# Three Newton rounds of the row norms moved from VectorE to GpSimd, for four of five gate batches

## The chip, the cores and the metric

The kernel runs on one core of one Trainium2 chip. The metric is device time in microseconds of one execution; the kernel before took 1360.23 us, the median of three runs (1359.64 to 1362.73). Engine names in the rows: PE is TensorE, PEld its weight loads, DVE is VectorE, ACT is ScalarE, POOL is GpSimd, SP is SyncE, which here issues DMAs.

## The reference

Three layers follow one another on 4608 tokens of width 512: attention inside chunks of 64 tokens, a mixture of eight experts in which each token goes to one, and a wide layer with a swish.

```python
scores = scale * np.matmul(q_c, k_c.transpose(0, 1, 2, 4, 3))
attn = softmax(scores)                       # rows of 64
x = concat_heads(np.matmul(attn, v_c))       # (4608, 512)

xn = x / (np.linalg.norm(x, axis=-1, keepdims=True) + 1e-06)
en = expert_emb / (np.linalg.norm(expert_emb, axis=-1, keepdims=True) + 1e-06)
logits = xn @ en.T / tau
expert_idx = np.argmax(logits, axis=1)
gate_w = softmax(logits)[np.arange(N), expert_idx]
out[mask] = gate_w[mask, None] * (np.maximum(x[mask] @ w1[e], 0.0) @ w2[e])   # per expert e

h = out @ w_in
result = (h * (1.0 / (1.0 + np.exp(-1.702 * h)))) @ w_out
```

The change concerns one quantity: 1 / (norm of x + 1e-6) for each token, by which its eight logits are scaled.

## The kernel before

Tokens are worked in 36 tiles of 128. The first stage, the attention, ends some 218 us into the span; the expert layer and the wide layer follow and fill the rest. In the attention stage a loop over n (L1143) is a software pipeline: in step n it makes scores and softmax of tile n (`emit_S`, `max_S`, `exp_S`), transposes the probabilities of tile n-1 (`emit_PT`, `evac_PT`), multiplies tile n-2 by v (`emit_PV`, `emit_x`), sums the squares of tile n-3 on ACT (`emit_sq`) and writes tile n-3 out in two halves of 16 bits (`emit_X`). The order is written by hand: each engine executes its instructions in the order in which the code issues them, and an instruction that waits holds everything behind it on that engine.

On DVE a step has the row maxima `mx` (L378), the subtraction `P` (L381), on some steps a copy `xTa` (L476), the scale of a tile (`si_all`, `sx_all`, L442 and L447), its high half `xr` (L452), and the normalised output `x` (`rd`, L424 and L426, then L428). On ACT a step has four evacuations of transposed q or k (`kuT`, `quT`, L349), the squares `sq` of an `x` (L436), sometimes a copy `xTa` (L474), `PT` (L401) and the exponential of `P` (L388). On POOL a step has two instructions of 128x512: the scaling of `x` (L454) and the low half `xr` (L455).

Routing is done in five batches of 8, 8, 8, 6 and 6 tiles (`batches`, L479). When the last tile of a batch has been through `emit_X`, `norm(bi)` is put into the queue `todo`; `gate(bi)` follows it there when the logits of the last tile are there. Both are generators, and `drip(1)`, which stands at about ten places of a step, takes one piece out of the queue's head, so that these small instructions lie between the large ones. With `rate` 2 (steps 29 to 32) it takes two. `norm` turns the sums of squares `ss_all` of a batch (128 x 8 numbers, or 128 x 6) into `rn_all`: a first guess by an integer shift and a subtraction, three Newton rounds of three instructions (`rsqrt`, L215), a product that turns 1/norm into norm, the 1e-6, a reciprocal, and a scaling. All 16 of these are DVE instructions, and a drip stands between any two.

A generator that yields "pe" is set aside once:

```python
        if g in paused:
            n -= paused.pop(g)
            continue
        ...
        if next(g) == "pe":
            paused[g] = 8
```

The next call of `drip` takes the 8 off its own allowance of one or two, removes the entry and ends; the call after that takes the generator's next piece.

Of the kernel before, what the change touches and what calls it, by code (L numbers as in the profile page):

```python
# [12 lines left out]
I32 = mybir.dt.int32  # L13
U32 = mybir.dt.uint32
AF = mybir.ActivationFunctionType
ALU = mybir.AluOpType
# [18 lines left out]
def kernel(  # L35
# [13 lines left out]
    nc = tc.nc  # L49
# [102 lines left out]
    for t in vt:  # L152
# [15 lines left out]
        out=tri16, in_=ones16, pattern=[[1, 128]], compare_op=ALU.is_gt, fill=0.0,  # L168
# [19 lines left out]
    for m_, op_ in ((lt_m, ALU.is_lt), (le_m, ALU.is_le)):  # L188
        nc.vector.tensor_tensor(
            out=m_, in0=io_e.unsqueeze(1).to_broadcast([128, NE, NE]),  # L190
            in1=io_e.unsqueeze(2).to_broadcast([128, NE, NE]), op=op_,
# [23 lines left out]
    def rsqrt(y, t, a, ssc):  # L215

        nc.vector.tensor_scalar(t, ssc.bitcast(I32), 1, None, op0=ALU.logical_shift_right)
        yield
        nc.vector.tensor_scalar(
            y.bitcast(I32), t, -1.0, 1597463007.0, op0=ALU.mult, op1=ALU.add  # L220
        )
        yield
        for _ in range(3):
            nc.vector.scalar_tensor_tensor(
                out=a, in0=y, scalar=-0.5, in1=ssc, op0=ALU.mult, op1=ALU.mult
            )
            yield
            nc.vector.tensor_tensor(out=a, in0=a, in1=y, op=ALU.mult)
            yield
            nc.vector.scalar_tensor_tensor(  # L230
                out=y, in0=a, scalar=1.5, in1=y, op0=ALU.add, op1=ALU.mult
            )
            yield
# [245 lines left out]
    batches = [(0, 8), (8, 8), (16, 8), (24, 6), (30, 6)]  # L479
# [19 lines left out]
    def small(nm, n, dt=F32, w=None, bufs=1):  # L499
        t = att.tile([128, 8] if w is None else [128, 8, w], dt, tag="g_" + nm, name="g_" + nm, bufs=bufs)  # L500
        return t[:, 0:n]
# [3 lines left out]
    def norm(bi):  # L505
        t0, n = batches[bi]
        ssc, y = ss_all[:, t0:t0 + n], rn_all[:, t0:t0 + n]
        yield from rsqrt(y, small("t", n, I32), small("a", n), ssc)
        nc.vector.tensor_tensor(out=y, in0=y, in1=ssc, op=ALU.mult)
        yield  # L510
        nc.vector.tensor_scalar(y, y, 1e-6, None, op0=ALU.add)
        yield
        nc.vector.reciprocal(out=y, in_=y)
        yield
        isx = is_all[:, t0:t0 + n]
        nc.vector.tensor_scalar(
            isx.bitcast(I32), si_all[:, t0:t0 + n], float((BIAS - X_TOP) << 23), None, op0=ALU.add
        )
        yield
        nc.vector.scalar_tensor_tensor(  # L520
            out=y, in0=y, scalar=itau[:, 0:1], in1=isx, op0=ALU.mult, op1=ALU.mult
        )
        yield
# [603 lines left out]
    def end_X(t):  # L1127
        emit_X(t)
        for bi, (t0, nn) in enumerate(batches):
            if t == t0 + nn - 1:  # L1130
                todo.append(norm(bi))
# [698 lines left out]
```

## Time and profile before

| | |
|---|---|
| median of three runs | 1360.23 us |
| profiled execution, span | 1360.5 us, 1358.8 us |
| attention stage, 26 to 218 us: DVE, ACT, PE, POOL busy | 157.00, 159.02, 143.13, 96.64 us of 192 |
| 600 to 1350 us: PE busy | 728.49 us of 750 |
| mean granted TensorE clock | 0.979 |

A timeline row gives start, duration, engine, line, operation, and in brackets how long the engine sat idle before it and what ended that. Lines are those of the kernel before. Where two DVE instructions don't depend on each other, the second can start a little before the first one's end.

### The profile page before, as it was taken

How to read it: one execution, taken by the hardware profiler on the slowest of the kernel's cores; microseconds unless marked ns; L12 is line 12 of the kernel's file. 1: busy time of each engine (PE TensorE's matmuls, PEld its weight loads, DVE VectorE, ACT ScalarE, POOL GpSimd, SP SyncE). 2: the span in 40 equal slices, each digit the busy share in tenths (PEclk: the TensorE clock that was granted, in tenths of full speed). 3: DMA queues.
4: the chain of work that ended last, by engine and by line, in shares of the span. 5: the costliest groups of instructions: out<-in, count | busy, mean ns of one | idle time of the engine just before them, and what ended most of it. 6: DMA issues, size and time to landing. Idle time of an engine off the chain costs nothing. (4 is left out here: it accounts for less than half of the span.)

```text
span 1358.8 us, 35354 instructions
## 1 busy us (share of the span) xinstructions
PE 1245.2 (92%) x14192; PEld 1026.7 (76%) x14192; DVE 1052.1 (77%) x1872; ACT 729.4 (54%) x1301; POOL 716.5 (53%) x652
## 2 busy tenths in 40 slices
PE   6778767899999999999899999999999999999997
PEld 4656656677666666667588888888888888888886
DVE  4688888778988878886678696968787796968681
ACT  7899865235544545454454545545454545455453
POOL 1455543142544254543157575766667675757664
PEclk9999978999999999999999999999999999999999
DMA  9999634668655759876507253443526062534413
GB/s 196 228 246 227 158 136 123 187 180 235 181 184 160 212 164 276 252 230 159 150 5 214 63 164 117 125 156 92 189 34 220 28 196 85 156 125 124 156 39 118
DMA packets 218455, 213.63 MB, mean 157 GB/s; under 512 B 127320, under 2 KB 171352, under 8 KB 218272
## 3 DMA queue, kind: packets, MB, share of 16 engines
q1 hardware_dynamic: 204880, 184.17, 50.6%
q0 software_dynamic: 6000, 19.67, 4.2%
q10 hardware_dynamic: 7392, 7.36, 1.7%
q8 instruction: 114, 1.87, 0.6%
q14 instruction: 69, 0.57, 0.1%
HBM read 154.98 MB, written 36.52 MB: 141 GB/s over the span
## 5 line engine op out<-in xcount | busy, mean ns | idle before, releaser
L1536 PEld LDWEIGHTS <-wS 128*128 128x128 f16 x3024 | 296.4, 98 | 54.7 <-issue 16.2
L1029 PEld LDWEIGHTS <-w1HL 128*128 128x128 f16 x3744 | 215.5, 99 | 26.4 <-DVEq L962 9.4
L1029 PE MATMUL ph<-xTm,w1HL 128*128 128x128 f16 x3744 | 221.8, 221 | 14.3 <-DVEq L962 8.0
L1064 PE MATMUL py<-w2HL,hT 128*128 128x512 f16 x912 | 204.7, 379 | 6.1 <-DVEq L962 3.4
L1064 PEld LDWEIGHTS <-hT 128*128 128x128 f16 x936 | 90.0, 98 | 109.8 <-issue 9.5
L1089 ACT ACTIVATE y<-py,ysc 128x512 f16<-128x512 f32 x38 | 26.1, 687 | 142.6 <-DVE ysc L1086 142.6
L1004 POOL DMA_INDIRECT xg<-xs,id_i x39 | 42.9, 1100 | 109.4 <-DMA xTm<-xg 75.3
L1536 PEld LDWEIGHTS <-w2HL 128*128 128x128 f16 x864 | 84.5, 98 | 10.6
L1536 PEld LDWEIGHTS <-w1HL 128*128 128x128 f16 x864 | 84.5, 98 | 9.8
L454 POOL TENSOR_TENSOR x<-x,sx_all 128x512 f32<-128x512 f32 x33 | 34.3, 1039 | 107.5 <-DVE rd L424 49.1
L1256 POOL TENSOR_TENSOR wS<-d_f,wS 128x512 f16<-128x512 f32 x28 | 36.5, 1319 | 73.9 <-ACT wS L1255 43.8
L1562 ACT ACTIVATE zA<-zA 128x512 f32<-128x512 f32 x72 | 45.3, 629 | 54.0 <-DVE zA L1559 31.4
L1403 POOL TENSOR_TENSOR w1HL<-zA,w1HL 128x512 f16<-128x512 f32 x36 | 48.5, 1346 | 43.5 <-ACT w1HL L1399 43.5
L1396 DVE TENSOR_TENSOR zA<-zA 128x512 f32<-128x512 f32 x72 | 65.6, 911 | 1.2
L1037 DVE SCALAR_TENSOR_TENSOR hT<-ph,hT 128x512 f16<-128x512 f32 x78 | 51.4, 684 | 16.7 <-ACT hT L1036 16.5
L1036 ACT ACTIVATE hT<-ph 128x512 f16<-128x512 f32 x78 | 44.2, 593 | 31.1 <-PE ph L1029 31.0
L1536 PE MATMUL pd<-stg,wS 128*128 128x256 f16 x456 | 54.7, 272 | 5.2 <-ACT stgB L1399 5.2
L1686 POOL DMA_INDIRECT out_dram<-hT,idc x36 | 35.4, 983 | 35.8 <-ACT hT L1681 32.8
L1536 PE MATMUL pa<-stg,wS 128*128 128x256 f16 x432 | 51.8, 273 | 2.6 <-ACT stgB L1399 2.6
L1536 PE MATMUL pb<-stg,wS 128*128 128x256 f16 x408 | 49.0, 272 | 3.9 <-ACT stgB L1399 3.9
L1090 DVE SCALAR_TENSOR_TENSOR y<-py,ysc,y 128x512 f16<-128x512 f32 x38 | 28.5, 751 | 28.7 <-ACT y L1089 28.7
L349 ACT ACTIVATE kuT<-tp 64x512 f32<-64x512 f32 x72 | 45.2, 627 | 9.0 <-PE tp L344 8.1
(408 smaller groups left out, 3138.7 us busy)
## 6 DMA issues: line engine op xcount, KB each, us to landing
ring<-wod SPq DMA_DIRECT2D x63, 1024.0 KB
stg<-in_moe_w_dram SPq DMA_DIRECT2D x14, 1024.0 KB
stgB<-in_moe_w_dram SPq DMA_DIRECT2D x14, 1024.0 KB
ys<-y SPq DMA_DIRECT2D x39, 258.0 KB
vt<-in_v_dram SPq DMA_DIRECT2D x64, 144.0 KB
xs<-xr SPq DMA_DIRECT2D x36, 256.0 KB
raw_o<-in_moe_w_in_dram SPq DMA_DIRECT2D x16, 512.0 KB
raw_o<-in_moe_w_out_dram SPq DMA_DIRECT2D x16, 512.0 KB
```

Source lines behind the costliest of these rows:

```text
L349: lambda r=r, p=p, dst=dst: nc.scalar.activation(out=dst[:, :, r], in_=p[r * 64:(r + 1) * 64], func=AF.Copy)
L1004: nc.gpsimd.indirect_dma_start(out=xg[:, :], out_offset=None, in_=src, in_offset=bass.IndirectOffsetOnAxis(ap=id_i[:, i:i + 1], axis=0),)
L1029: nc.tensor.matmul(p[:, f % 4], wt[:, c, fs], xT[:, a, :], start=(c == 0 and a == 0 and wt is w1H), stop=(c == KD - 1 and wt is w1L),)
L1036: nc.scalar.activation(out=hi, in_=p, func=AF.Relu)
L1037: nc.vector.scalar_tensor_tensor(out=lo, in0=p, scalar=0.0, in1=hi, op0=ALU.max, op1=ALU.subtract)
L1064: nc.tensor.matmul(p, hT[:, a, :], wt[:, c, :], start=st, stop=sp)
L1256: nc.gpsimd.tensor_tensor(out=L_, in0=f, in1=H_, op=ALU.subtract)
L1396: nc.vector.tensor_tensor(out=o, in0=x, in1=p, op=op)
L1403: eng.tensor_tensor(out=lo, in0=x, in1=hi, op=ALU.subtract)
L1536: nc.tensor.matmul(dst, lhs(a, k, ab), rhs(b, k), start=first and ab == abs_[0] and k == 0 and m == 0, stop=(k == n - 1 and m == 2), skip_ ...
L1562: nc.scalar.activation(out=z, in_=z, func=AF.Sigmoid, scale=1.702 * 2.0 ** -G_EXP)
L1686: disjoint("out", nc.gpsimd.indirect_dma_start(out=out[:, :], out_offset=bass.IndirectOffsetOnAxis(ap=id_t[j][0][:, 2 * h + t, 0:1], axis= ...
```

## The change

For all batches the scaling factor `is_all` is made first instead of last. For the four first batches `norm` makes the first guess on DVE and then issues, in one piece, fifteen POOL instructions: `h` = -ss/2, three rounds of four (the fused DVE forms become separate ones), the product with `ss_all` and the 1e-6. Then it yields "pe", and the reciprocal and the scaling follow on DVE. The last batch keeps its Newton rounds on DVE.

```diff
     def norm(bi):
         t0, n = batches[bi]
         ssc, y = ss_all[:, t0:t0 + n], rn_all[:, t0:t0 + n]
-        yield from rsqrt(y, small("t", n, I32), small("a", n), ssc)
-        nc.vector.tensor_tensor(out=y, in0=y, in1=ssc, op=ALU.mult)
-        yield
-        nc.vector.tensor_scalar(y, y, 1e-6, None, op0=ALU.add)
-        yield
-        nc.vector.reciprocal(out=y, in_=y)
-        yield
         isx = is_all[:, t0:t0 + n]
         nc.vector.tensor_scalar(
             isx.bitcast(I32), si_all[:, t0:t0 + n], float((BIAS - X_TOP) << 23), None, op0=ALU.add
         )
+        yield
+        if bi + 1 < len(batches):
+            gp = nc.gpsimd
+            t, a, h = small("t", n, I32), small("a", n), small("h", n)
+            nc.vector.tensor_scalar(t, ssc.bitcast(I32), 1, None, op0=ALU.logical_shift_right)
+            yield
+            nc.vector.tensor_scalar(y.bitcast(I32), t, -1.0, 1597463007.0, op0=ALU.mult, op1=ALU.add)
+            gp.tensor_scalar(h, ssc, -0.5, None, op0=ALU.mult)
+            for _ in range(3):
+                gp.tensor_tensor(out=a, in0=h, in1=y, op=ALU.mult)
+                gp.tensor_tensor(out=a, in0=a, in1=y, op=ALU.mult)
+                gp.tensor_scalar(a, a, 1.5, None, op0=ALU.add)
+                gp.tensor_tensor(out=y, in0=y, in1=a, op=ALU.mult)
+            gp.tensor_tensor(out=y, in0=y, in1=ssc, op=ALU.mult)
+            gp.tensor_scalar(y, y, 1e-6, None, op0=ALU.add)
+            yield "pe"
+        else:
+            yield from rsqrt(y, small("t", n, I32), small("a", n), ssc)
+            nc.vector.tensor_tensor(out=y, in0=y, in1=ssc, op=ALU.mult)
+            yield
+            nc.vector.tensor_scalar(y, y, 1e-6, None, op0=ALU.add)
+            yield
+        nc.vector.reciprocal(out=y, in_=y)
         yield
```

On DVE before, the first batch's norm begins behind the high half of tile 7 (step 10); `g_t`, `g_a` and `rn_all` are the norm's, `rd`, `x` and `mx` the tiles':

```order
L217 TENSOR_SCALAR g_t<-ss_all 128x8
L219 TENSOR_SCALAR rn_all<-g_t 128x8
L424 TENSOR_SCALAR rd<-db 128x8
L224 SCALAR_TENSOR_TENSOR g_a<-rn_all,ss_all 128x8
L426 RECIPROCAL rd<-rd 128x8
L228 TENSOR_TENSOR g_a<-g_a,rn_all 128x8
L428 TENSOR_TENSOR x<-db,rd 128x2x4x64
L230 SCALAR_TENSOR_TENSOR rn_all<-g_a,rn_all 128x8
L224 SCALAR_TENSOR_TENSOR g_a<-rn_all,ss_all 128x8
L378 TENSOR_REDUCE mx<-sp_178 128x8
```

The same place of DVE in the changed kernel:

```order
L509 TENSOR_SCALAR is_all<-si_all 128x8
L516 TENSOR_SCALAR g_t<-ss_all 128x8
L424 TENSOR_SCALAR rd<-db 128x8
L518 TENSOR_SCALAR rn_all<-g_t 128x8
L426 RECIPROCAL rd<-rd 128x8
L428 TENSOR_TENSOR x<-db,rd 128x2x4x64
L534 RECIPROCAL rn_all<-rn_all 128x8
L536 SCALAR_TENSOR_TENSOR rn_all<-rn_all,itau,is_all 128x8
L378 TENSOR_REDUCE mx<-sp_178 128x8
```

The norm's reciprocal (L534) now stands in step 10, two instructions behind the piece that hands the rounds over (L518) and ahead of the next step's `mx`; before, it stood a step later. Batches two and three have the same order.

On POOL in the changed kernel, the place behind the low half of tile 7 (the names in brackets are the engines whose work the instruction waits for):

```order
L455 TENSOR_TENSOR xr<-x,xr 128x512 [waits DMAHW2_49,PE_49,Pool_49]
L519 TENSOR_SCALAR g_h<-ss_all 128x8
L521 TENSOR_TENSOR g_a<-g_h,rn_all 128x8 [waits DVE_49,Pool_49]
L522 TENSOR_TENSOR g_a<-g_a,rn_all 128x8 [waits Pool_49]
L523 TENSOR_SCALAR g_a<-g_a 128x8 [waits Pool_49]
L524 TENSOR_TENSOR rn_all<-rn_all,g_a 128x8 [waits Pool_49]
```

Two more such rounds, the product and the sum follow, each with the same wait, and then the scaling of tile 8 (L454). Before, L454 of tile 8 followed L455 of tile 7 directly.

On DVE before, the fourth batch (step 32, two pieces to a drip):

```order
L217 TENSOR_SCALAR g_t<-ss_all 128x6
L219 TENSOR_SCALAR rn_all<-g_t 128x6
L224 SCALAR_TENSOR_TENSOR g_a<-rn_all,ss_all 128x6
L228 TENSOR_TENSOR g_a<-g_a,rn_all 128x6
L424 TENSOR_SCALAR rd<-db 128x8
L230 SCALAR_TENSOR_TENSOR rn_all<-g_a,rn_all 128x6
L224 SCALAR_TENSOR_TENSOR g_a<-rn_all,ss_all 128x6
L426 RECIPROCAL rd<-rd 128x8
```

The same place in the changed kernel:

```order
L509 TENSOR_SCALAR is_all<-si_all 128x6
L516 TENSOR_SCALAR g_t<-ss_all 128x6
L518 TENSOR_SCALAR rn_all<-g_t 128x6
L424 TENSOR_SCALAR rd<-db 128x8
L534 RECIPROCAL rn_all<-rn_all 128x6
L536 SCALAR_TENSOR_TENSOR rn_all<-rn_all,itau,is_all 128x6
L426 RECIPROCAL rd<-rd 128x8
L428 TENSOR_TENSOR x<-db,rd 128x2x4x64
```

Here the norm's reciprocal stands ahead of the tile's own `rd` and `x`. The orders of PE, ACT and SP are the same in both kernels.

## Rows read from the trace of the kernel before

**Rows 1.** Windows: start:end, length, busy us by engine, clock, DMA share, GB/s.
```profile
26.00:218.00 192.00, 143.13 (x3223) 117.17 (x3221) 157.00 (x493) 159.02 (x296) 96.64 (x99) 0.90 0.89 200
600.00:1350.00 750.00, 728.49 (x6699) 635.51 (x6697) 567.66 (x761) 378.78 (x676) 464.83 (x400) 1.00 0.43 127
```
**Rows 2.** Timeline of ACT, step 11 and the beginning of step 12.
```profile
70.49 0.62 ACT L388 ACTIVATE P<-P 128x512 f32<-128x512 f32 x1
...
72.68 0.63 ACT L436 ACTIVATE sq<-x 128x512 f32<-128x512 f32 x1 [0.39 <-DVE x L428]
```
**Rows 3.** Timeline of DVE, steps 8 to 12.
```profile
53.43 0.68 DVE L378 TENSOR_REDUCE mx<-sp 128x8 f32<-128x512 f32 x1
...
58.31 0.69 DVE L378 TENSOR_REDUCE mx<-sp 128x8 f32<-128x512 f32 x1 [1.60 <-PE sp L371]
...
61.51 0.69 DVE L428 TENSOR_TENSOR x<-db,rd 128x512 f32<-128x512 f32 x1
62.75 0.69 DVE L378 TENSOR_REDUCE mx<-sp 128x8 f32<-128x512 f32 x1 [0.55 <-PE sp L371]
...
64.45 0.49 DVE L452 TENSOR_SCALAR xr<-x,sx_all 128x512 f16<-128x512 f32 x1
...
65.26 0.89 DVE L224 SCALAR_TENSOR_TENSOR g_a<-rn_all,ss_all 128x8 f32<-128x8 f32 x1
...
67.59 0.69 DVE L378 TENSOR_REDUCE mx<-sp 128x8 f32<-128x512 f32 x1
...
71.72 0.20 DVE L513 RECIPROCAL rn_all<-rn_all 128x8 f32<-128x8 f32 x1
...
72.97 0.23 DVE L520 SCALAR_TENSOR_TENSOR rn_all<-rn_all,itau,is_all 128x8 f32<-128x8 f32 x1
73.11 0.69 DVE L378 TENSOR_REDUCE mx<-sp 128x8 f32<-128x512 f32 x1
```
**Rows 4.** Timeline of POOL: the tile before the first and the fourth batch's norm.
```profile
65.08 1.04 POOL L454 TENSOR_TENSOR x<-x,sx_all 128x512 f32<-128x512 f32 x1 [1.57 <-DVE g_t L217]
66.20 1.18 POOL L455 TENSOR_TENSOR xr<-x,xr 128x512 f16<-128x512 f32 x1
...
186.19 1.17 POOL L455 TENSOR_TENSOR xr<-x,xr 128x512 f16<-128x512 f32 x1
```
**Rows 5.** POOL by line: count, shortest/median/longest ns; then two of the timeline.
```profile
L1264 POOL TENSOR_TENSOR d_f<-d_f x16: 1262/1275/1397, 281.9 to 440.3; 128x512 f32<-128x512 f32 x16
L1264 POOL TENSOR_TENSOR d_f<-fo,d_f x16: 722/758/1594, 466.4 to 625.4; 128x256 f32<-128x256 f32 x16
L629 POOL TENSOR_SCALAR raw_o<-io_k,slot x32: 590/602/1637, 88.1 to 232.6; 128x128 f16<-128x128 f16 x32
...
2.22 0.13 POOL L174 IOTA io_e_i<- 128x8 int32 x1
2.31 0.13 POOL L174 IOTA io_re_i<- 128x8 int32 x1
```
**Rows 6.** A DVE product of the norm, by line, columns as in the last group.
```profile
L228 DVE TENSOR_TENSOR g_a<-g_a,rn_all x15: 156/166/168, 66.2 to 223.4; 128x8 f32<-128x8 f32 x9, 128x6 f32<-128x6 f32 x6
```
**Rows 7.** Timeline of DVE, step 33.
```profile
192.39 0.69 DVE L428 TENSOR_TENSOR x<-db,rd 128x512 f32<-128x512 f32 x1
```
**Rows 8.** Timelines and one window, 97 to 106 us: a late transfer and what follows.
```profile
97.61 0.48 DVE L452 TENSOR_SCALAR xr<-x,sx_all 128x512 f16<-128x512 f32 x1 [3.56 <-DMA xs<-xr]
99.26 0.70 PE L416 MATMUL db<-vt,PT 64*64 64x65 f32 x32 [1.63 <-DVE x L428]
99.30 0.63 ACT L436 ACTIVATE sq<-x 128x512 f32<-128x512 f32 x1 [1.59 <-DVE x L428]
100.00:104.00 4.00, 3.57 (x56) 2.91 (x56) 2.79 (x8) 3.93 (x8) 2.40 (x3) 0.57 1.14 246
106.02 1.02 ACT L474 ACTIVATE xTa<-sp 128x1024 f16<-128x1024 f16 x1 [0.51 <-PE tp L344]
```
**Rows 9.** Timeline of ACT, step 32.
```profile
188.68 0.63 ACT L436 ACTIVATE sq<-x 128x512 f32<-128x512 f32 x1 [1.24 <-DVE g_a L224]
```

## The prediction

> **What bounds the kernel now.** I read the windows first: they say which stage is full and of what. In the attention stage ACT is busy 159 of 192 us and DVE 157, both ahead of PE; in the last 750 us PE is busy 97% [rows 1]. The reader is to see two things: the edited instructions all lie in the stage where ACT and DVE carry the time, and the stages behind it are full of PE work, so that an attention stage which ends later ends the kernel later by the same amount.
>
> Next the timelines of ACT and DVE around the first norm (steps 10 to 12). ACT works without a gap until it starts the squares of a tile, where it waits 0.39 us for DVE's `x` [rows 2]. So ACT sets the pace, and DVE is only just behind it where a norm lies among its work. An ordinary step of DVE takes 3.89 us from the start of `mx` to the end of the `x` that ACT squares next (58.31 to 61.51 + 0.69); with the norm among it, the steps from 62.75 to 73.11 take 10.36 us, where the two before them (53.43 to 62.75) took 9.32 [rows 3]. Hence the norm costs some 1.0 us per batch today, and that is all that an edit of it can give back there.
>
> The third view is POOL's timeline: in step 10 it begins the scaling of tile 7 at 65.08, 0.14 us after DVE's `xr` ended (64.45 + 0.49) [rows 3, 4], and is done with the low half at 67.38. The gap between its two instructions, of which the second needs the first, is 0.08 us [rows 4].
>
> **What is removed.** Eleven DVE instructions per batch for four batches, three rounds of three, the product and the sum; 0.17 us each where nothing holds them [rows 6]. One of the first stands at 65.26 for 0.89 us, until POOL's scaling has ended at 66.12 [rows 3, 4]: some of the norm's DVE time is waiting for POOL. Moving `is_all` to the front costs nothing: it is the same instruction, issued once.
>
> **What is added, and where.** The piece that hands over is followed on DVE by the tile's reciprocal and its `x`, and then by the norm's reciprocal, which needs the last of POOL's fifteen instructions. The pause does not keep them a step apart: it costs one call of `drip`, and in the changed order the reciprocal stands ahead of the `mx` of step 11. What is queued behind it on DVE is that `mx`, then `P`, the copy `xTa` and the next `x`; ACT's exponential waits for `P`, PE's next scores for `P` and the logits for `xTa`. In front of POOL's chain stand the two large instructions of tile 7, which end at 67.38, while DVE is there at 67.1 or so. DVE thus waits for the whole chain.
>
> The chain's length L is the term that the trace doesn't show, because no POOL instruction of this size with two inputs exists. The nearest are the two forms of L1264: 722 ns for 256 columns and 1262 ns for 512 at their shortest, which is 2.11 ns a column and 182 ns without any; for 8 columns that makes 0.20 us [rows 5]. Every one waits for the one before it, so the gap of 0.08 us comes on top [rows 4]. I take 0.28 us for each of the fifteen, the five with one input too, and L = 4.2 us. From below: two independent fills of 128x8 start 0.09 us apart and take 0.13 [rows 5]; 15 x 0.09 = 1.3 us if the chain ran without any gap, 15 x (0.13 + 0.08) = 3.2 us with it. From above: the one-input form with 128 columns takes 0.60 us [rows 5]; 15 x (0.60 + 0.08) = 10.2 us. L below the 0.28 or so that DVE arrives before POOL would cost nothing; no row comes near that.
>
> A page speaks against this edit. The Trainium skill, "GPSIMD Engine Reference", section "Engine selection", says to keep elementwise work on VectorE because GpSimd is about twice as slow with two inputs. A DVE product of the norm takes 0.166 us [rows 6]; no row shows the same on POOL. By that page an estimate for one is 2 x 0.166 + 0.08 = 0.41 us, L would be 6.2 us, and by the sum below the time would be 1382.5 us.
>
> **The sum, batch one.** POOL's chain starts at 67.38 + 0.08 = 67.46 and ends at 71.66; DVE is released 0.14 later, at 71.80. The reciprocal (0.20) and the scaling (0.23) end at 72.23 [rows 3], where `mx` starts; before, it started at 67.59 [rows 3]. With no norm left among it the step needs 3.89 us to the end of `x`, 76.1, and ACT squares it 0.1 later, at 76.2. Before, that was 72.68 [rows 2]: 3.5 us later. ACT cannot use the time: its exponential of tile 11, at 70.49 before, needs the `P` that comes out 4.6 us late, and everything stands behind it. Batches two and three stand at the same place of their steps with the same distances, so 3 x 3.5 = 10.5 us.
>
> **Batch four.** With two pieces to a drip the norm's reciprocal stands even ahead of the tile's own. POOL is through with the tile at 186.19 + 1.17 = 187.36 [rows 4]; the chain ends at 191.64, DVE goes on at 191.78, and two reciprocals, the scaling and `x` (0.20 + 0.23 + 0.20 + 0.69) end at 193.1. Then 3.89 us to the end of the next `x`, 197.0; before 192.39 + 0.69 = 193.08 [rows 7]. That is 3.9 us.
>
> **What is given back, what else is lost.** At 97.61 DVE had waited 3.56 us for a store of `xr` to land, and ACT 1.59 us for the `x` behind it [rows 8]. The store and the loads before it keep the DMA queues full through the stage (share 0.89 [rows 1]), so I expect it to land when it did; a pipeline that comes 3.5 us late finds it there, and 1.6 us of batch one are given back. No later transfer holds ACT in this stage. On the other side, behind that wait PE had been idle 1.63 us, the clock granted from 100 to 104 us was 0.57, between its lower level (1.2 GHz) and the full one (2.4 GHz), and at 106.02 ACT waited 0.51 us for PE's transposes [rows 8]. Each of the new stalls leaves PE without work for longer than that, so I add 0.5 us for each of the first three; at the fourth the clock changes anyway.
>
> Sum: 10.5 + 3.9 - 1.6 + 1.5 = 14.3 us. The profiled execution took 1360.5 us, its span 1358.8; it would be 1373.1 in span and 1374.8 in all. It stands 0.3 us above the median of the runs, so the forecast is 1360.23 + 14.3 = 1374.5 us. Every microsecond of L counts four times.
>
> **Rivals.**
> - No change. If POOL's short instructions follow one another as the fills do, L is 1.3 us; each of three batches costs 0.6 us, the fourth 1.0, of which 0.6 is given back at 97 us, and the clock keeps its level: +2.2 us, 1362.4 us. For it: those fills overlap. Against it: they don't depend on each other, and each new instruction waits for the one before. It decides below L of about 1.4 us.
> - Faster. The chain ends before DVE gets to the reciprocal; then DVE is rid of the norm, the 1.0 us per batch goes three times, and ACT's wait of 1.24 us behind the fourth [rows 9]: -4.3 us, 1355.9 us. For it speaks the 0.89 us of one small instruction held by POOL [rows 3]. The Trainium skill, "SBUF — State Buffer", section "SBUF: two separate sides", has that as a lock which one of DVE and GpSimd holds for a whole instruction; by that rule, and the trace agrees in that row, DVE instructions of this kind are better off elsewhere. Against it: the chain can't start before 67.46, and DVE is at the reciprocal by then. It needs L under 0.7 us, less than half of the smallest bound.
> - Much slower. If each of the fifteen takes what L629 takes, L is 10.2 us and the time 1360.23 + 14.3 + 4 x 6.0 = 1398.5 us. Against it: L629 has sixteen times the columns. It counts from L = 7 us.
>
> **How the numbers follow.** Forecast (L from about 1.6 to 7 us): 0.80. No change: 0.08. Faster: 0.05. Much slower: 0.07. Around the forecast, L = 1.6 to 7 gives 1364 to 1386 us, and this is the range; it leaves out the other three. Runs of this kernel tell 0.2%, 2.7 us, from nothing; so faster by more than that 0.05, the same 0.10 (the no-change case and the edge of the forecast), slower 0.85.
>
> **What would show it.** Right: DVE idle before the norm's reciprocal (L534) four times, for L + 0.3 or so, ended by POOL L526; fifteen POOL instructions in a row at 0.28 us from start to start; the `mx` behind each over 4 us late, ACT idle before its exponential by some 3 us; the attention stage some 14 us longer and the rest as before. The wait at 97 us gone. Wrong: the reciprocal without a wait; POOL's steps well under 0.2 us or over 0.45; or a stage that takes up the stall, as it would if the DMA queues, not ACT and DVE, set the pace over more of it than the one wait shows: then up to batch three would be given back, and the time would be nearer to 1368.

## The result, and the profile after

The changed kernel took 1372.72 us, the median of five runs (1372.14 to 1377.55), against 1360.43 us for the kernel before in the same job (1359.64 to 1362.73): a ratio of 1.0111, 95% interval 1.0097 to 1.0125. The ratio stands for 15.1 us; the two medians alone differ by 12.3. The forecast was 1374.5 us, with a range of 1364 to 1386. The profiled execution of the changed kernel took 1376.4 us, span 1374.6, one of the two longest of the five; what sets those two apart from the other three was not found.

The windows come first, as before [rows 1]; columns are start:end, length, busy us of PE, PEld, DVE, ACT and POOL, granted clock, DMA share, GB/s.

```profile
26.00:218.00 192.00, 140.47 (x3072) 115.15 (x3073) 138.17 (x405) 150.25 (x280) 101.37 (x150) 0.86 0.81 183
600.00:1350.00 750.00, 729.01 (x6753) 634.28 (x6750) 579.06 (x777) 382.78 (x680) 466.96 (x398) 1.00 0.44 129
```

In the same window the two engines that carry the attention stage are less busy, DVE by 18.8 us and ACT by 8.8, and POOL is busier by 4.7. Part of DVE's fall is the 44 instructions taken off it; the rest of both falls is work that the window no longer reaches. No engine is busier by the size of the loss; so it is idle time. The last 750 us are as full of PE work as before. The view of what DVE waits for (total us, times, longest) and the same for ACT name the idle time:

```profile
DVE rn_all L534 <- POOL rn_all L526: 19.7, 4, 5.5
```
```profile
ACT P L388 <- DVE P L381: 8.9, 3, 3.0
```

The timelines show the first of the four. DVE, steps 10 to 12, against [rows 3]:

```profile
65.69 1.02 DVE L518 TENSOR_SCALAR rn_all<-g_t 128x8 int32<-128x8 int32 x1
66.92 0.69 DVE L428 TENSOR_TENSOR x<-db,rd 128x512 f32<-128x512 f32 x1
72.36 0.20 DVE L534 RECIPROCAL rn_all<-rn_all 128x8 f32<-128x8 f32 x1 [4.75 <-POOL rn_all L526]
72.60 0.23 DVE L536 SCALAR_TENSOR_TENSOR rn_all<-rn_all,itau,is_all 128x8 f32<-128x8 f32 x1
72.74 0.68 DVE L378 TENSOR_REDUCE mx<-sp 128x8 f32<-128x512 f32 x1
...
203.70 0.19 DVE L534 RECIPROCAL rn_all<-rn_all 128x6 f32<-128x6 f32 x1 [5.54 <-POOL rn_all L526]
```

POOL's timeline of the same stretch, against [rows 4]; the fifteen instructions lie between 67.90 and 72.32:

```profile
66.77 1.17 POOL L455 TENSOR_TENSOR xr<-x,xr 128x512 f16<-128x512 f32 x1
67.90 0.27 POOL L519 TENSOR_SCALAR g_h<-ss_all 128x8 f32<-128x8 f32 x1
68.25 0.21 POOL L521 TENSOR_TENSOR g_a<-g_h,rn_all 128x8 f32<-128x8 f32 x1
68.53 0.21 POOL L522 TENSOR_TENSOR g_a<-g_a,rn_all 128x8 f32<-128x8 f32 x1
68.83 0.26 POOL L523 TENSOR_SCALAR g_a<-g_a 128x8 f32<-128x8 f32 x1
69.17 0.20 POOL L524 TENSOR_TENSOR rn_all<-rn_all,g_a 128x8 f32<-128x8 f32 x1
...
72.09 0.23 POOL L526 TENSOR_SCALAR rn_all<-rn_all 128x8 f32<-128x8 f32 x1
```

And ACT, against [rows 2]: the exponential of tile 11 ran at 70.49 before.

```profile
70.60 0.60 ACT L401 ACTIVATE PT<-ptp 128x512 f32<-128x512 f32 x1
74.19 0.63 ACT L388 ACTIVATE P<-P 128x512 f32<-128x512 f32 x1 [2.99 <-DVE P L381]
...
76.65 0.63 ACT L436 ACTIVATE sq<-x 128x512 f32<-128x512 f32 x1 [0.68 <-DVE x L428]
```

The chain ends at 72.32, DVE's reciprocal starts at 72.36, and everything in line behind it on DVE and then on ACT moves back. How the delay adds up is seen from the start of `mx` (L378) in the same step of both traces. The last column is the change since the row above; before the first norm the two traces already differ by 0.56 us.

| step | before | after | later by | change |
|---|---|---|---|---|
| 10 | 62.75 | 63.31 | 0.56 | |
| 12 (behind batch 1) | 73.11 | 77.19 | 4.08 | +3.5 |
| 16 | 92.40 | 96.40 | 4.00 | -0.1 |
| 18 (behind the late store) | 104.24 | 105.63 | 1.39 | -2.6 |
| 20 (behind batch 2) | 114.51 | 119.44 | 4.93 | +3.5 |
| 26 | 143.70 | 149.31 | 5.61 | +0.7 |
| 28 (behind batch 3) | 154.06 | 163.12 | 9.06 | +3.5 |
| 32 | 182.74 | 194.69 | 11.95 | +2.9 |
| 33 (behind batch 4) | 188.98 | 204.91 | 15.93 | +4.0 |
| 35 | 201.24 | 216.75 | 15.51 | -0.4 |

### The profile page after: what moved, and what is told of

Its sections match the earlier page's. It is cut to its first block, busy times and chain, and to the rows that moved or that the text cites. A ratio compares the mean times of both kernels' runs of the same rounds, so it can differ in the third digit from the quotient of the medians.

```text
span 1374.6 us, 35366 instructions
## 1 busy us (share of the span) xinstructions
PE 1251.1 (91%) x14192; PEld 1032.7 (75%) x14192; DVE 1042.0 (76%) x1828; ACT 730.1 (53%) x1301; POOL 729.7 (53%) x712
## 5 line engine op out<-in xcount | busy, mean ns | idle before, releaser
L1045 PE MATMUL ph<-xTm,w1HL 128*128 128x128 f16 x3744 | 221.8, 221 | 14.3 <-DVEq L978 7.6
L454 POOL TENSOR_TENSOR x<-x,sx_all 128x512 f32<-128x512 f32 x33 | 34.3, 1041 | 105.4 <-DVE rd L424 64.5
L378 DVE TENSOR_REDUCE mx<-sp 128x8 f32<-128x512 f32 x36 | 24.8, 688 | 36.2 <-PE sp L371 35.5
L349 ACT ACTIVATE kuT<-tp 64x512 f32<-64x512 f32 x72 | 45.1, 627 | 10.7 <-PE tp L344 9.8
```

The source lines that it names most:

```text
L349: lambda r=r, p=p, dst=dst: nc.scalar.activation(out=dst[:, :, r], in_=p[r * 64:(r + 1) * 64], func=AF.Copy)
L1045: nc.tensor.matmul(p[:, f % 4], wt[:, c, fs], xT[:, a, :], start=(c == 0 and a == 0 and wt is w1H), stop=(c == KD - 1 and wt is w1L),)
```

## The experiments

Theory A, that of the prediction: DVE stands in line behind POOL's chain, and its queue and ACT's move back by what the chain is late. Rival B: POOL's extra work itself costs the time, by holding DVE's or its own large instructions up. Rival C, for the size: the DMA queues or the stall as such set the loss, not the chain's length.

**The changed kernel again** (after_again), beside the next three on one chip.

> The changed kernel unaltered, run again beside the others. Its five runs lie in two clusters, 1372.1 to 1372.7 us and 1376.4 to 1377.6 us, and the trace at hand is of the upper one (1376.4 us, DVE waits before the norm's reciprocal 4.75, 4.69, 4.69 and 5.54 us). Theory A (DVE stands in line behind GpSimd's chain) expects the four waits again at 4.7 to 5.6 us, 19 to 20 us in sum, in whichever cluster the run falls, and 1371 to 1378 us. A rival, that the clusters come from the waits themselves, expects the sum of the waits to differ by about 4 us between the clusters.

Measured: 1373.77 us, the kernel before 1359.33; ratio 1.010 [1.008, 1.012]. The four waits of L534 sum to 19.6 us, as theory A has it. The run that was traced took 1376.36 us, again the longest of its job, so the rival on the clusters is not tested: no trace shows a run near 1372 us.

**The reciprocal half a step later** (late8).

```diff
-            yield "pe"
+            for _ in range(8 * rate[0]):
+                yield
```

> The norm's reciprocal comes eight pieces later (eight empty yields in place of the pause; 16 in the fourth batch), behind the high half of the next tile; GpSimd's chain is as in the changed kernel. Theory A: DVE arrives at the reciprocal some 3 us later, at about 70.4 us in the first batch, while the chain ends at about 72.3; a wait of about 1.9 us is left per batch, the norm's own eleven instructions are gone, and the time is 1361 to 1366 us. Theory B (the fifteen instructions cost by holding GpSimd's port and by making the scaling of the next tile late): the order of DVE does not matter and the time stays at 1370 us or above.

Measured: 1362.77 us, ratio 1.0020 [1.0007, 1.0033]. The reciprocal, now line 535, stands behind the next tile's `xr` and still waits, four times, 6.3 us in all. The first:

```profile
70.84 0.49 DVE L452 TENSOR_SCALAR xr<-x,sx_all 128x512 f16<-128x512 f32 x1
72.92 0.20 DVE L535 RECIPROCAL rn_all<-rn_all 128x8 f32<-128x8 f32 x1 [1.59 <-POOL rn_all L526]
```

The same fifteen instructions on POOL and the same work taken off DVE, and four fifths of the loss are gone (2.7 of 13.6 us stay, by the ratios) with two thirds of the wait. So the place of the wait in DVE's order makes the loss. This speaks for A against B.

**The reciprocal a whole step later** (late14; taken again in more rounds as late14_again).

```diff
-            yield "pe"
+            for _ in range(14 * rate[0]):
+                yield
```

> As the run before with fourteen empty yields (28 in the fourth batch): the reciprocal stands behind the row maxima of the step after next. Theory A: the chain has ended when DVE gets there, no wait is left, and DVE is rid of eleven instructions per batch: 1355 to 1360 us, faster than the kernel before by up to 4.3 us. Theory B: 1370 us or above.

> The hand-over with the reciprocal put 14 empty pieces later instead of the pause (28 in the fourth batch), taken again in more rounds. Theory (chain hidden, VectorE rid of the Newton rounds, 1.0 us gained per batch and partly taken back by waits for stores): no wait before the reciprocal, 1 to 3 us under the kernel before, ratio 0.998 to 0.9995. Rival (what is gained per batch is all taken back by the stores): ratio 1.000 within 0.0010.

Measured: 1357.57 us, ratio 0.9985 [0.9971, 1.0000], and again 1357.24 against 1359.94 us, ratio 0.9985 [0.9970, 0.9999]. No wait is left before the reciprocal; it ran straight behind `mx` of step 12 (DVE of late14_again):

```profile
72.24 0.69 DVE L378 TENSOR_REDUCE mx<-sp 128x8 f32<-128x512 f32 x1 [0.56 <-PE sp L371]
72.85 0.19 DVE L535 RECIPROCAL rn_all<-rn_all 128x8 f32<-128x8 f32 x1
72.97 0.69 DVE L381 TENSOR_TENSOR P<-sp,mx 128x512 f32<-128x512 f32 x1
...
75.26 0.49 DVE L452 TENSOR_SCALAR xr<-x,sx_all 128x512 f16<-128x512 f32 x1 [0.51 <-DMA xs<-xr]
...
97.42 0.48 DVE L452 TENSOR_SCALAR xr<-x,sx_all 128x512 f16<-128x512 f32 x1 [3.27 <-DMA xs<-xr]
```

This version beats both kernels, the one before by 0.15%, which the two jobs only just tell from nothing. The three first norms bring `mx` forward by 1.07 us each (steps 11 to 12, 19 to 20, 27 to 28), as the prediction read off [rows 3], the fourth by 1.8. At step 35 only 0.7 of these 5.0 us are left (from 0.20 later at step 10 to 0.48 earlier). Of the fourth norm's 1.8 us, 1.5 are gone by step 35: there ACT waits 0.86 us for a load of weights (`stg`, at 191.14 us) and DVE for ACT. Another 1.3 us are missing between steps 28 and 32, where the trace of the kernel before is the fastest of all ten (table below). And DVE now reaches some stores too early, as in the rows at 75.26 and 97.42: such waits before L452 sum to 5.9 us in four places, against 4.9 in three before. The medians differ by 2.7 us, more than the stage shows; the rest was not traced.

**POOL's work without anyone waiting for it** (pool_beside): the kernel before, with as many POOL instructions on scratch tiles.

```diff
+        if bi + 1 < len(batches):
+            gp = nc.gpsimd
+            z, az, h = small("z", n), small("az", n), small("h", n)
+            gp.tensor_scalar(h, ssc, -0.5, None, op0=ALU.mult)
+            gp.tensor_scalar(z, ssc, 0.5, None, op0=ALU.mult)
+            for _ in range(3):
...
+            gp.tensor_tensor(out=z, in0=z, in1=ssc, op=ALU.mult)
```

> The kernel before, with fifteen GpSimd instructions of the same kinds and sizes added at the same four places, on scratch tiles that nobody reads (the result is that of the kernel before; these rounds start from another number). DVE keeps its norm. Theory A: nobody waits for the chain except the scaling of the next tile, which comes about 1.7 us late and is not urgent; 1359 to 1364 us. Theory B: most of the 12 us come with the fifteen instructions alone: 1368 us or above.

Measured: 1361.55 us, ratio 1.0013 [0.9997, 1.0029]. POOL's work alone costs between nothing and 4 us, not the 13.6 or 15: rival B falls as the main cause. It is not nothing, though. In this trace the steps across each of the first three norms take 0.8 to 0.9 us longer than before (table below), because POOL's two large instructions of the next tile, 71.39 to 72.43 and 72.51 to 73.67 us, come later and two small DVE instructions of the norm last until each of them has ended (before, they took 0.43 and 0.23 us):

```profile
71.51 0.95 DVE L527 TENSOR_SCALAR is_all<-si_all 128x8 int32<-128x8 int32 x1
72.50 1.20 DVE L531 SCALAR_TENSOR_TENSOR rn_all<-rn_all,itau,is_all 128x8 f32<-128x8 f32 x1
```

In the changed kernel POOL's next large instruction starts only at 75.67 us, behind the whole norm.

**One batch at a time** (only_b1, only_b3).

```diff
-        if bi + 1 < len(batches):
+        if bi == 0:     # only_b1; in only_b3: bi == 2
```

> The hand-over to GpSimd for the first batch alone; the other four keep their rounds on VectorE. Theory (VectorE stands in line for the GpSimd chain, and a wait for a late store, which the kernel before has at 97 us, takes some of it back): one wait of about 4.7 us before the reciprocal; the row maxima of the following steps 4 to 5 us later than before up to step 16, and only 1.4 to 2.5 us later from step 18 on, because the store that VectorE waited 3.56 us for lands when it did; the time 1.4 to 2.5 us above the kernel before. Rival (each batch costs the same quarter of the whole loss): 3 to 3.5 us above, and the row maxima keep their full delay past step 18.

> The hand-over for the third batch alone. Theory: one wait of about 4.7 us; the row maxima agree with the kernel before up to step 26, are 4 to 5 us late from step 27 on, and nothing takes it back before the stage ends: 3.5 to 4.5 us above the kernel before, ratio about 1.003. Rival (the DMA queues set the pace of the stage and take the stall up): under 1.5 us above, row maxima level again by step 33.

Measured: only_b1 1360.81 us, ratio 1.0009 [0.9998, 1.0021], that is +1.2 us (-0.3 to 2.9); only_b3 1362.51 us, ratio 1.0028 [1.0013, 1.0043], +3.8 us (1.8 to 5.8). Each trace has one wait of 4.7 us before L534. In only_b1 `mx` is 3.46 us later than before at step 16 and 0.85 at step 18: 2.6 us are taken back at the late store. (That trace was 1.58 us ahead at step 10, so its own delay is 5.0, then 2.4.) DVE's `xr` of that step had waited 3.56 us [rows 8]; here it waits for no transfer (its 1.42 us run beside POOL's low half of the tile before, 97.61 to 98.76):

```profile
97.62 1.42 DVE L452 TENSOR_SCALAR xr<-x,sx_all 128x512 f16<-128x512 f32 x1
100.65 0.69 DVE L378 TENSOR_REDUCE mx<-sp 128x8 f32<-128x512 f32 x1 [0.49 <-PE sp L371]
```

In only_b3 `mx` agrees with before to 0.43 us at step 26, is 3.88 us later at step 28 and 5.70 at step 35: nothing of the 3.5 us comes back. The growth behind step 28 does not belong to the stall: only_b1, which has none there, grows by 1.4 us over the same steps. By these rows the rival of equal quarters falls for batch one, and that of the DMA queues for batch three. The two times, 1.2 and 3.8 us, point the same way, but their intervals overlap.

**A longer chain** (four_rounds).

```diff
-            for _ in range(3):
+            for _ in range(4):
```

> The changed kernel with a fourth Newton round on GpSimd: 19 chained instructions instead of 15, the rest the same. Theory (each microsecond of the chain counts once per batch): the chain grows by 4 x 0.29 = 1.2 us, each of the four waits from 4.7 to 5.9 us (the last 6.7), and the time is 4 to 4.7 us above the changed kernel, about 1377.5 us, ratio to the kernel before 1.0135. Rival (the loss comes from the stall as such, the lower clock and what restarts, and hardly from its length): within 1.5 us of the changed kernel, 1372 to 1375 us.

Measured: 1375.89 us, ratio 1.0125 [1.0105, 1.0145]. The waits grew as expected, from 19.7 to 24.3 us:

```profile
DVE rn_all L534 <- POOL rn_all L526: 24.3, 4, 6.7
```

`mx` of step 12 is 1.15 us later than in the changed kernel's trace, each counted from its own step 10, and that of step 35 is 3.3 us later (18.23 against 14.95). Against the second trace of the changed kernel (after_again) step 35 is 4.3 us later (18.23 against 13.96), and at the four norms themselves the longer chain costs 1.15, 1.18, 1.18 and 1.16 us more than in the changed kernel's first trace, 4.7 in all, as the theory has it. So by the traces a longer chain costs again at each batch, and rival C falls; the 3.3 comes of steps 28 to 32, where the first trace was slow. The run times alone can't tell the two: by the ratios 1.9 us above the changed kernel's first job and 3.4 above its second, each uncertain by 3 to 4.

**All ten traces side by side.** Time in us from the start of `mx` in one step to that in another. The first four columns span the four norms; from step 16 to 18 lies the late store; the last column has no Newton rounds in it. In late8 and both late14 the reciprocal of the fourth norm has moved out of its column.

| run | 10 to 12 | 18 to 20 | 26 to 28 | 32 to 33 | 16 to 18 | 28 to 32 |
|---|---|---|---|---|---|---|
| before | 10.36 | 10.27 | 10.36 | 6.24 | 11.84 | 28.68 |
| after | 13.88 | 13.81 | 13.81 | 10.22 | 9.23 | 31.57 |
| after_again | 13.85 | 13.79 | 13.78 | 10.19 | 9.25 | 29.24 |
| four_rounds | 15.03 | 14.99 | 14.99 | 11.38 | 9.25 | 29.36 |
| late8 | 11.28 | 11.27 | 11.29 | 4.41 | 10.53 | 31.23 |
| late14 | 9.30 | 8.89 | 9.29 | 4.41 | 11.61 | 30.03 |
| late14_again | 9.29 | 9.28 | 9.27 | 4.42 | 10.67 | 30.02 |
| pool_beside | 11.18 | 11.14 | 11.16 | 6.24 | 9.22 | 30.46 |
| only_b1 | 14.07 | 10.13 | 10.14 | 6.24 | 9.23 | 30.33 |
| only_b3 | 10.13 | 10.15 | 13.81 | 6.24 | 10.53 | 30.50 |

What a norm costs comes out nearly the same in every trace of one order. The last column does not follow the change at all.

## Why the prediction was right

- **The queue.** Right: DVE arrives before POOL's chain begins, waits for all of it at four places, and ACT waits 2.99 us before its exponential. That this makes the loss is shown by late8 and late14, where the same chain runs and the loss shrinks with the wait, and by four_rounds, where both grow with the chain.
- **L, 4.2 us.** Measured 72.32 - 67.90 = 4.4. The two-input instructions took 0.20 to 0.21 us, as the two widths of L1264 gave [rows 5], and 0.28 to 0.30 from start to start. The one-input ones took 0.23 to 0.27, up to 0.35 from start to start: these make the 0.2 us. From the end of the chain to DVE's start 0.04 us passed, not the 0.14 of the sum. The Trainium skill, "GPSIMD Engine Reference", section "Engine selection", had given an estimate of 0.41 us each and 1382.5 us in all; that was too high, since a product took 0.20 us here against 0.166 on DVE [rows 6]. Its advice to keep such work on VectorE held for this edit, though not for its reason: in late14 the same instructions on POOL cost no time, because nobody waits for them.
- **3.5 us per batch.** Measured +3.5 in each of the first three, in both traces of the changed kernel.
- **Batch four, 3.9 us.** Measured +4.0, of which 0.4 came back by step 35.
- **Given back, 1.6 us.** Measured 2.6, and the reason given for it is not borne out. The trace before had two things there, DVE's wait of 3.56 us and behind it a clock of 0.57 [rows 8]; late14 has both too (2.97 us and 0.70). late8, late14_again and only_b3 wait as long, 3.13 to 3.27 us, and keep the full clock. From step 16 to 18 these three take 10.5 to 10.7 us, the two with the lower clock 11.6 and 11.8, and the runs with little or no wait 9.2. So the wait that is gone gave back 1.3 to 1.4 us, about what was forecast; the rest, some 1.2, goes with the lower clock, which the trace before had there and others with the same wait did not. The changed kernel has no wait there and the full clock of 2.4 GHz (the third row; windows of after, columns as above):

```profile
72.00:76.00 4.00, 1.20 (x19) 1.00 (x19) 3.43 (x11) 1.77 (x3) 0.57 (x3) 0.84 1.15 269
76.00:80.00 4.00, 4.00 (x86) 3.28 (x86) 3.20 (x9) 3.29 (x6) 2.35 (x3) 0.74 1.09 220
100.00:104.00 4.00, 3.21 (x83) 2.57 (x81) 2.71 (x7) 3.93 (x9) 1.75 (x2) 1.00 0.89 230
...
170.00:174.00 4.00, 2.33 (x45) 1.95 (x44) 3.20 (x11) 1.15 (x3) 1.57 (x2) 0.53 0.02 4
```

The same window in late14_again, behind a wait of 3.27 us:

```profile
100.00:104.00 4.00, 3.19 (x84) 2.60 (x85) 3.41 (x10) 3.95 (x8) 2.40 (x3) 1.00 1.22 250
```

The prediction expected the store to land when it did, so that whoever comes 3.5 us later finds it there. In late8 DVE came 2.5 us later than before (step 16) and still waited 3.13 us; in pool_beside it came 0.85 us later and waited 0.70, until 95.60. The landing itself lies 2 us later in the one and 2 us earlier in the other; what moves it was not found.

```profile
99.69 0.48 DVE L452 TENSOR_SCALAR xr<-x,sx_all 128x512 f16<-128x512 f32 x1 [3.13 <-DMA xs<-xr]
```

- **The clock, 0.5 us for each of three stalls.** Not shown. The clock does fall behind the first stall (0.84 and 0.74 above, against 1.00 before), but no stretch shows a loss that goes with them. Behind batch one (steps 12 to 16) the changed kernel's first trace lost nothing and its second 1.3 us, but only_b3, without a stall by then, is 1.1 longer too. Of the 0.7 behind batch two only_b3 has as much. Behind batch three (28 to 32) the first trace lost 2.9 us, with the clock near its lower level of 1.2 GHz in places (0.53 of the full 2.4 GHz from 170 to 174 us). But there the trace before is the fastest of all ten: only_b1 and pool_beside, with no stall at batch three, are 1.7 and 1.8 us longer, after_again and four_rounds, which have one, only 0.6 and 0.7. No run held the clock up; what the stalls cost by it stays open.
- **The sum.** 14.3 us; the two traces have 15.0 and 14.0 at step 35, the two jobs 15.1 and 13.6 by their ratios. The four stops make 14.5 and 14.4 of it, where the forecast had 14.4: this is the mechanism, and it was right in size at each of the four places. The two small terms were luck. They were to cancel, at -1.6 and +1.5; measured are -2.6 in both traces, and 3.1 and 2.2 in all other stretches together, of which no part is shown to belong to the change.
- **The rivals.** Much slower and no change fell with L. The faster one asked for a chain that ends before DVE gets there; late14 made that so, and brought 2.0 us (by its ratio) of the 4.3 reckoned: the DVE time was there, 1.07 us at each of three norms, and waits for loads and stores took part of it.

## What to carry to other kernels

Work handed to an idle engine makes its owner wait unless the instruction that fetches the result stands behind at least the chain's length of other work in the owner's own queue; count that distance in the order of the instructions, not in what a pause is called. Price a chain as its steps times the start-to-start time of one, and multiply by how often the queue stops. When a stall is added, look downstream for a wait for a transfer that it swallows. And before a microsecond of some stretch is put down to the change, look at that stretch in runs where the change does not touch it: here the trace before was the odd one in steps 28 to 32, by 1.3 us or more against every run without a stall there.

## What the runs showed of the hardware

- On POOL a 128x8 instruction with one input and a constant took 0.23 to 0.27 us, longer than one with two inputs (0.20 to 0.21), and 128x6 took as long as 128x8. In the fourth batch:

```profile
199.61 0.21 POOL L521 TENSOR_TENSOR g_a<-g_h,rn_all 128x6 f32<-128x6 f32 x1
199.90 0.20 POOL L522 TENSOR_TENSOR g_a<-g_a,rn_all 128x6 f32<-128x6 f32 x1
200.19 0.25 POOL L523 TENSOR_SCALAR g_a<-g_a 128x6 f32<-128x6 f32 x1
```

- Moving the rounds away does not end the holding of small DVE instructions: L518 lasted 1.02 us in the changed kernel, until POOL's scaling of the tile had ended at 66.69, and in late14_again the norm's last scaling took 0.92 us, until POOL's low half had ended at 74.48, where it took 0.23 in the kernel before [rows 3].
